# Row maxima of the first phase in small groups inside the matmul tasks, in an adaptive-norm block with softmax attention

## The chip, the cores and the metric

The kernel runs on one core of a Trainium2 chip. The metric is the device time of one execution in microseconds; lower is better. TensorE is called PE, VectorE DVE, ScalarE ACT, GpSimd POOL, and SP is the engine that issues most DMAs.

## What is computed

A block with adaptive layer norm on 2048 tokens of width 448: a softmax attention of 16 heads (28 wide each), then an MLP of width 1792, both scaled and shifted by rows made from a conditioning vector. All of it is in float32.

```python
mod = (_silu(c) @ w_mod).reshape(c.shape[0], 6, 1, -1)
sa, ca, ga, sb, cb, gb = (mod[:, i] for i in range(6))
h = _layernorm(x) * (1 + ca) + sa
q, k, v = split(h @ wqkv)                      # 16 heads of 28
p = _softmax(q @ k^T * 28 ** -0.5)             # 2048 x 2048 per head
x = x + ga * ((p @ v) @ wo)
h = _layernorm(x) * (1 + cb) + sb
x = x + gb * (gelu(_layernorm(h) @ w1 + b1) @ w2 + b2)
```

## The kernel before

**Precision.** Each float32 operand is split into a high and a low part, and a product is three products of parts. A projection of 448 input channels is therefore eleven accumulating matmuls (`terms448`, issued by `mm_acc`).

**Two phases of attention.** The first phase makes queries, keys and values; the second makes scores, exponentials and the weighted sums. The softmax needs a maximum of each row before the exponentials. It is not found from the final scores, but ahead of them, from a product of the high parts alone: for group `g` of four heads, query tile `qt` (512 queries), key block `cch` (512 keys), a quarter `i` of the queries (128) and head `j`, `max_mm` multiplies 128 queries by 512 keys (L466) into one PSUM buffer, and DVE reduces that to one column (`max_one`, L471). There are 1024 such maxima. Head `j` uses rows 32j to 32j+27 of the PE array, its *row group*, so matmuls of four different `j` run at the same time.

When all 64 maxima of a query tile are there (`count`, with the counter `left`), `max_fin` reduces them and later a call `put` transposes them on DVE (L509) and writes them by four DMAs (L512) into an extra row of the query tile, beside the 28 rows of each head. The score matmuls of that tile (L1162) read that row, so the maximum is subtracted by the matmul itself.

**Pairs.** For the first group of heads and query tiles 1 to 3, the key blocks 0 and 1 are taken together: `pair_diff` multiplies the queries by the difference of the two key blocks (`k_diff`), ACT applies a Relu to that (L479) into one of three tiles of slot `d0`, and a second matmul with key block 0 (`rest`) is combined with it on DVE (L483). So one pair takes two matmuls, one ACT read and one DVE read and gives two maxima. There are 48 pairs.

**The order of the first phase.** It runs over four blocks `b` of 512 tokens, and in each over a list of tasks: query and key projections (`qk_task`), value projections (`v_task`), each eleven matmuls into one of two `pa` buffers, and between them the transposes and the affine step of the next block (`h_chunk`, L267) and, in block 1, the modulation matmuls (L630). The order of every engine's instructions is the order in which this code issues them. Maxima that have become possible wait in two lists: `mxq` for single ones, `pxq` for pairs. They are sorted so that those of head group 0 and query tile 0 come first, then head group 1, then the rest of group 0.

The maxima are issued by `emit_task` behind each task: four or five operations, sometimes a sixth (`P1RATE`, `p1_n`), with both matmuls of one to three pairs in the same call. In five tasks `emit_mid` issues four more halfway through the eleven matmuls. Their PSUM buffers are a ring of five (`mx_ring`: two `ma`, two `m2`, one `m1`); a sixth operation uses the buffer `o`.

**The border.** Behind the loop's last task (the sixteenth value projection is left for attention step 0) `finish_max(0, 0)` issues whatever maxima the first query tile still lacks, and `tick_late(True)` calls its `put`. Then the PSUM pools are changed over and the second phase starts. It has 256 steps (16 units of head group and query tile, 16 key tiles each), and each step issues the remaining maxima too (`emit_max`), three or four per step by the rule in `n_maxima`. In the last four units, steps 8 to 11 also carry part of the output projection; there the number follows from how many maxima are left over.

Of the kernel before, what the change touches and what calls it, by code (L numbers as in the profile page):

```python
# [26 lines left out]
NC = 4  # L27
# [2 lines left out]
NKT = S // 128  # L30
NFT = F // 128
NTT = S // 128
P1RATE = 4
YTAGS = [f"{a}{i}" for a in ("kh", "qh") for i in range(4)]
EPS = 1e-5
SCALE = float(DH) ** -0.5
# [3 lines left out]
def tile_adaln_block(ctx: ExitStack, tc: tile.TileContext, x, wqkv, wo, w1, b1, w2, b2, c, w_mod, out):  # L40
# [338 lines left out]
            )  # L379
        sp.dma_start(ones_d.rearrange("j (q n) -> j q n", n=256), ones[:, None, :].broadcast_to([4, 8, 256]))  # L380

    def mm_acc(p, terms, mid=None):
        for i, (a, b) in enumerate(terms):
            if mid and i == len(terms) // 2:
                mid()
            pe.matmul(p, a, b, start=(i == 0), stop=(i == len(terms) - 1))  # L386


# [16 lines left out]
    def qk_task(b, kind, g, begun=None):  # L405
        p, ts = begun or qk_terms(b, kind, g)
        if begun is None:
            mm_acc(p, ts, p1_n[3])
        emit_task(*p1_n[:3])
        if g == 0:  # L410
            tg = ("kh" if kind else "qh") + str(b)
            hi = sb.tile([128, 512], F32R, tag=tg, name=nm(tg), bufs=1)
            (kh_sb if kind else qh_sb)[(g, b)] = hi
        elif g == 1 and b < 2:

            hi = sbt("raw" if kind else "osb", [128, 512], F32R, bufs=3 if kind else 2)
            (kh_sb if kind else qh_sb)[(g, b)] = hi
        else:
            hi = sbt("hi", [128, 512], F32R, bufs=3)
        full = sbt("full", [128, 512], bufs=3)  # L420
        lo = sbt("lo", [128, 512], F32R, bufs=3)
        act.copy(full, p)

        def split():
            (act.copy if b else dve.tensor_copy)(hi, full)
            if kind == 1 and (g, b) == (0, 1):
                k_diff.append(sbt("raw", [128, 512], F32R, bufs=3))
                pool.tensor_tensor(out=k_diff[0], in0=f(hi), in1=f(kh_sb[(0, 0)]), op=ALU.subtract)
            pool.tensor_tensor(out=lo, in0=full, in1=f(hi), op=ALU.subtract)
            sl = slice(b * 512, (b + 1) * 512)  # L430
            for part, t in enumerate((hi, lo)):
                sp.dma_start(f(dscr[kind][part][g])[:, sl], f(t))

            if b < 3 or g == 0 or (kind, g) == (0, 1):
                put_spare()
            spare.append((kind, g, sl))

        return split

    def v_task(b, t, p):  # L440
        ts = slice(t * 128, (t + 1) * 128)
        hh, hl = hT[b]
        mm_acc(p[:, :D], terms448(
            lambda k: hh(k)[:, ts], lambda k: hl(k)[:, ts], lambda k: wv[0][:, k, :], lambda k: wv[1][:, k, :],
        ), p1_n[3] if phase1[0] else None)
        if phase1[0]:
            emit_task(*p1_n[:3])
        act.copy(v_sb[b][:, t, :, :DH], p[:, :D].rearrange("p (h d) -> p h d", d=DH))


# [2 lines left out]
    mxq = []  # L453
    pxq = []
# [68 lines left out]
    phase1 = [True]  # L523
# [49 lines left out]
            count(g, qt, [cch])  # L573


    def emit_task(n, sixth, n_pairs):
        if not n:
            return
        pairs = [pxq.pop(0) for _ in range(min(n_pairs, len(pxq)))]
        rests = [pair_diff(*m) for m in pairs]  # L580
        js = [m[3] for m in pairs]
        n_ops = n - len(pairs) + (sixth and len(pairs) > 0)
        singles = []
        for x in range(n_ops - len(pairs)):
            if mxq:

                free = [j for j in range(4) if j not in js] or range(4)
                fits = [y for y, m in enumerate(mxq[:16]) if m[:3] == mxq[0][:3] and m[4] == free[x % len(free)]]
                singles.append(mxq.pop(fits[0] if fits else 0))
        ops = [lambda ps, m=m: max_one(*m, ps) for m in singles]  # L590
        ops[2:2] = rests
        for x, op in enumerate(ops):
            op(ps_o if x + len(pairs) == 5 else ps_mx)
        for g, qt, cch, i, j in singles:
            count(g, qt, [cch])
        for g, qt, i, j in pairs:
            count(g, qt, [0, 1])


    def emit_mid():  # L600
        for j in range(4):
            fits = [x for x, m in enumerate(mxq[:16]) if m[4] == j]
            if fits:
                m = mxq.pop(fits[0])
                max_one(*m)
                count(*m[:2], [m[2]])

    p1_n = [0, False, 1, None]

    def finish_max(g, qt):  # L610
        while left[(g, qt)] > 0:
# [72 lines left out]
    for n, i in (  # L684
# [7 lines left out]
        p, ts = firsts[n]  # L692
# [3 lines left out]
    for b in range(NB):  # L696
        more = b + 1 < NB
        tasks = []
# [10 lines left out]
        for n, (tb, kind, g) in enumerate(tasks):  # L709
            post = []  # L710
            ready, newq = newq, []
            if not more and n == len(tasks) - 2:

                mx_ring[:] = ["ma", "ma", "m2", "m2", "m1"]
            p1_n[0] = P1RATE if b < 1 else P1RATE + 1
            if not more and n == len(tasks) - 1:
                p1_n[0] = 0

            k = n - (6, 4, 4, 4)[b]
            p1_n[1] = not (more and (0 <= k < NC)) and not (b == 1 and n < 4)  # L720
            p1_n[2] = (3 if n > 4 else 1) if b == 3 else 2 if b == 2 and p1_n[1] else 1
            p1_n[3] = emit_mid if (b, n) in ((1, 1), (1, 3), (1, 5), (1, 7), (2, 8)) else None
            if kind < 2:
                fn = qk_task(tb, kind, g, firsts[n] if b == 0 and n < 3 else None)
                if g == 0:
# [571 lines left out]
```

## Time and profile before

| | |
|---|---|
| median of 3 runs | 1129.84 us (1128.42 to 1130.21) |
| the profiled execution's own time | 1130.08 us |
| its span, first to last instruction | 1128.0 us |
| first phase, from its first full task to the first score matmul | 24.54 to 169.21 us |
| attention steps | 169.21 to 834 us |
| MLP | 834 us to the end |

The page gives busy time per engine, a row of tenths over the span, the chain of work that ended last, and groups of instructions by line of the source, engine and tile. The order of time shows single instructions or merged rows of equal ones: start, time from the first one's start to the last one's end, engine, line, operation, tile written and tiles read, and in brackets the idle time ahead of it and what ended that. `PE` rows are matmuls and `PEld` rows the weight loads that belong to them; matmuls overlap, so the distance from start to start is what one costs in a row of them.

### The profile page before, as it was taken

To read this page: it belongs to the slowest core of one execution; us is meant where nothing else is said; L and a number is where in the kernel's file an instruction comes from. 1 tells how busy PE (TensorE), PEld (TensorE's weight loads), DVE (VectorE), ACT (ScalarE), POOL (GpSimd) and SP (SyncE) were. 2 spreads that over 40 slices of the span, in tenths; PEclk is the share of its full clock that TensorE was granted. 3 is DMA by queue.
4 is the path that set the end of the run, shared out by engine and by line. 5 is a ranking of instruction groups with operands and counts; after the bars stand their busy time and mean duration, and the time that the engine had idled before them with its cause. 6 is when DMAs were issued, how large, how long until landed. Compare 5 with 4: busy or idle time off the path is not lost.

```text
span 1128.0 us, 20665 instructions
## 1 busy us (share of the span) xinstructions
PE 1116.4 (99%) x8319; PEld 670.1 (59%) x8319; DVE 843.7 (75%) x1485; ACT 672.0 (60%) x823; POOL 209.6 (19%) x211
## 2 busy tenths in 40 slices
PE   8999999999999999999999999999999999999998
PEld 6756674444444444444444454545468888888887
DVE  6968788999999999999999978595448853444322
ACT  4555657888887888788788867576752321111110
POOL 1533332110000000000000020217114504123000
PEclk9999999999999999999999999999999999999999
DMA  9562263121121211311111312020422100000000
GB/s 303 202 200 88 91 200 114 48 84 41 58 95 57 58 40 57 91 53 58 53 44 58 112 41 83 4 85 1 137 73 78 35 33 1 1 33 1 33 1 33
DMA packets 49341, 81.19 MB, mean 72 GB/s; under 512 B 12311, under 2 KB 18702, under 8 KB 49234
## 3 DMA queue, kind: packets, MB, share of 16 engines
q1 hardware_dynamic: 48762, 79.14, 22.1%
q8 instruction: 65, 1.06, 0.4%
q10 hardware_dynamic: 148, 0.46, 0.1%
q0 software_dynamic: 336, 0.28, 0.1%
q14 instruction: 30, 0.25, 0.1%
HBM read 55.04 MB, written 26.48 MB: 72 GB/s over the span
## 4 chain that ended last, share of the span: by engine, by line
PE 94%; DVE 3%; ACT 1%; DMA 1%; issue 1%; POOL 0%; SPq 0%; DVEq 0%; ACTq 0%; POOLq 0%
PE s L1162 26%; PE o L1132 22%; PE m L386 16%; PE pa L386 8%; PE m L466 6%; PE s L1232 3%; PE s L1233 3%; PE s L1231 3%; DVE mxp L471 2%; PE t L1232 1%; PE t L1233 1%; PE t L1231 1%; DMA slot_c<-in_w_mod_dram 1%; PE ma L466 1%; PE o L267 1%
## 5 line engine op out<-in xcount | busy, mean ns | idle before, releaser
L471 DVE TENSOR_REDUCE mxp<-m 128x1 f32<-128x512 f32 x884 | 568.8, 686 | 75.3 <-PE m L466 41.1
L1162 PE MATMUL s<-slot_b,slot_a 28*128 28x512 f32 (+1 forms) x3072 | 376.3, 420 | 0.0
L1162 PEld LDWEIGHTS s<-slot_b,slot_a 28*128 28x128 f32 (+1 forms) x3072 | 213.0, 184 | 247.4 <-ACT slot_c L1167 124.1
L466 PE MATMUL m<-kh,qh 28*128 28x512 f32 x863 | 287.6, 472 | 1.2 <-DVE mxp L471 0.9
L1167 ACT ACTIVATE slot_c<-s 128x1024 f32<-128x1024 f32 x170 | 174.3, 1025 | 75.9 <-PE s L1162 75.6
L1132 PE MATMUL o<-slot_c,v 128*32 128x512 f32 x680 | 178.8, 605 | 0.0
L1208 ACT ACTIVATE full<-m,b_col 128x512 f32<-128x512 f32 x56 | 38.6, 689 | 192.0 <-PE m L386 175.5
L1132 PE MATMUL o<-slot_c1h,v 128*32 128x512 f32 x512 | 134.7, 605 | 0.0
L1132 PE MATMUL o<-slot_c0h,v 128*32 128x512 f32 x512 | 134.7, 605 | 0.0
L1167 ACT ACTIVATE slot_c0h<-s 128x1024 f32<-128x1024 f32 x128 | 130.4, 1019 | 2.4 <-PE m L386 2.4
L1167 ACT ACTIVATE slot_c1h<-s 128x1024 f32<-128x1024 f32 x128 | 130.4, 1019 | 0.0
L1211 DVE CAST hi<-full 128x512 fp32r<-128x512 f32 x56 | 25.5, 455 | 134.6 <-ACT full L1208 134.6
L466 PEld LDWEIGHTS m<-kh,qh 28*128 28x128 f32 x863 | 114.3, 182 | 8.6 <-DVE mxp L471 5.1
L1167 ACT ACTIVATE slot_d<-s 128x1024 f32<-128x1024 f32 x86 | 88.1, 1025 | 39.3 <-PE s L1162 39.1
L895 POOL TENSOR_TENSOR osb<-osb,osb 128x512 f32<-128x512 f32 x16 | 20.9, 1307 | 441.1 <-DMA osb<-drec 356.8
L1132 PE MATMUL o<-slot_d,v 128*32 128x512 f32 x344 | 90.5, 605 | 0.4 <-ACT osb L1101 0.4
L386 PE MATMUL m<-y,slot_a 128*128 128x512 f32 x160 | 60.7, 395 | 0.0
L1132 PEld LDWEIGHTS o<-slot_c,v 128*32 128x32 f32 x680 | 24.5, 108 | 52.4 <-issue 49.5
L1212 DVE TENSOR_TENSOR lo<-full,hi 128x512 fp32r<-128x512 f32 x56 | 44.2, 788 | 5.9 <-DVE hi L1211 0.9
L471 DVE TENSOR_REDUCE mxp<-ma 128x1 f32<-128x512 f32 x54 | 35.6, 683 | 7.1 <-PE m L466 4.8
L386 PE MATMUL m<-y,slot_v 128*128 128x512 f32 x112 | 39.2, 396 | 0.0
L386 PE MATMUL m<-y,slot_b 128*128 128x512 f32 x112 | 39.0, 398 | 0.0
(316 smaller groups left out, 1626.7 us busy)
## 6 DMA issues: line engine op xcount, KB each, us to landing
slot_b<-d SPq DMA_DIRECT2D x32, 256.0 KB
slot_a<-d SPq DMA_DIRECT2D x32, 256.0 KB
d<-lo SPq DMA_DIRECT2D x28, 256.0 KB
d<-hi SPq DMA_DIRECT2D x16, 256.0 KB
osb<-drec SPq DMA_DIRECT2D x15, 256.0 KB
out_dram<-xn SPq DMA_DIRECT2D x16, 224.0 KB
raw<-in_B_w_dram SPq DMA_DIRECT2D x14, 224.0 KB
qh<-d SPq DMA_DIRECT2D x12, 256.0 KB
```

The source lines that it names most:

```text
L386: pe.matmul(p, a, b, start=(i == 0), stop=(i == len(terms) - 1))
L466: pe.matmul(m, qh_sb[(g, qt)][js, i * 128 : (i + 1) * 128], k[js, :], start=True, stop=True)
L471: dve.tensor_reduce(out=mxp[(g, qt)][:, i, j, cch : cch + 1], in_=m, op=ALU.max, axis=AX.X)
L1132: pe.matmul(o[32 * j : 32 * j + 32, :], v_sb[kt // 4][:, kt % 4, 4 * g + j, :], p[j // 2][:, j % 2, :], start=(kt == 0), stop=(kt == NKT - 1),
L1162: pe.matmul(s2[:, jj, :], ks[rows_, kp, kc], qs[rows_, qp, :], start=(term == 0), stop=(term == 2))
L1167: act.activation(pt[hf], s2, AF.Exp, scale=SCALE)
L1208: act.activation(gf, p, AF.Gelu_apprx_tanh, bias=b1_col[:, i : i + 1])
L1211: dve.tensor_copy(ghi, gf)
L1212: dve.tensor_tensor(out=glo, in0=gf, in1=f(ghi), op=ALU.subtract)
L1231: pe.matmul(pp, ghi[:, ts], w_hi, start=(m == 0), stop=False)
L1232: pe.matmul(pp, ghi[:, ts], w_lo, start=False, stop=False)
L1233: pe.matmul(pp, glo[:, ts], w_hi, start=False, stop=(m == NFT - 1))
```

## The change

`emit_task`, `emit_mid` and their rates are replaced. `emit_visit` issues at most one maximum per row group: first the second matmuls of the pairs that the last visit opened, counted as taken row groups, then up to two new pairs (three open or closing at a time), then single maxima for the row groups that are left. `visit_due` is called ahead of every matmul of a task's eleven and makes a visit once six (while pairs are waiting or open) or nine (otherwise) matmuls have passed. In a visit the new pairs' difference matmuls are issued first, then the second matmuls of the older pairs, then the single ones. The loop's last task but one opens no new pairs, and the last has no visits.

```diff
-P1RATE = 4
+PAIR_GAP, ONE_GAP = 6, 9
...
-    def mm_acc(p, terms, mid=None):
+    def mm_acc(p, terms, visits=False):
         for i, (a, b) in enumerate(terms):
-            if mid and i == len(terms) // 2:
-                mid()
+            if visits:
+                visit_due()
             pe.matmul(p, a, b, start=(i == 0), stop=(i == len(terms) - 1))
...
         if begun is None:
-            mm_acc(p, ts, p1_n[3])
-        emit_task(*p1_n[:3])
+            mm_acc(p, ts, True)
...
-        ), p1_n[3] if phase1[0] else None)
-        if phase1[0]:
-            emit_task(*p1_n[:3])
+        ), phase1[0])
...
-    def emit_task(n, sixth, n_pairs):
-        if not n:
-            return
-        pairs = [pxq.pop(0) for _ in range(min(n_pairs, len(pxq)))]
-        rests = [pair_diff(*m) for m in pairs]
...
-    def emit_mid():
+    px_open = []
+
+    def emit_visit(n_new):
+        rests = px_open[:]
+        px_open.clear()
+        js = [m[3] for m, _ in rests]
+        for _ in range(min(n_new, 3 - len(rests))):
+            fits = [x for x, m in enumerate(pxq[:8]) if m[3] not in js]
+            if fits:
+                m = pxq.pop(fits[0])
+                js.append(m[3])
+                px_open.append((m, pair_diff(*m)))
+        for (g, qt, i, j), rest in rests:
+            rest(ps_mx)
             count(g, qt, [0, 1])
         for j in range(4):
             fits = [x for x, m in enumerate(mxq[:16]) if m[4] == j]
-            if fits:
+            if fits and j not in js:
                 m = mxq.pop(fits[0])
                 max_one(*m)
                 count(*m[:2], [m[2]])
 
-    p1_n = [0, False, 1, None]
+    p1_n = [0, 0]
+
+    def visit_due():
+        p1_n[1] += 1
+        if p1_n[0] is not None and p1_n[1] > (PAIR_GAP if pxq or px_open else ONE_GAP):
+            p1_n[1] = 1
+            emit_visit(p1_n[0])
...
-            p1_n[0] = P1RATE if b < 1 else P1RATE + 1
-            if not more and n == len(tasks) - 1:
-                p1_n[0] = 0
-            k = n - (6, 4, 4, 4)[b]
-            p1_n[1] = not (more and (0 <= k < NC)) and not (b == 1 and n < 4)
-            p1_n[2] = (3 if n > 4 else 1) if b == 3 else 2 if b == 2 and p1_n[1] else 1
-            p1_n[3] = emit_mid if (b, n) in ((1, 1), (1, 3), (1, 5), (1, 7), (2, 8)) else None
+            p1_n[0] = (2, None if n == len(tasks) - 1 else 0)[not more and n >= len(tasks) - 2]
```

The lines of the code move by some three to twelve: what is L466, L471, L479, L483, L502, L509, L512, L1132 and L1162 before is L463, L468, L476, L480, L499, L506, L509, L1120 and L1150 after. L386 stays.

More of the change, by code (lines that the diff above doesn't have):

```diff
@@ L573, in emit_max @@
             count(g, qt, [cch])
-    def emit_task(n, sixth, n_pairs):
-        if not n:
-            return
-        pairs = [pxq.pop(0) for _ in range(min(n_pairs, len(pxq)))]
-        rests = [pair_diff(*m) for m in pairs]
[L581 to L596, printed above, removed]
+    px_open = []
[11 more added lines that the diff above has]
+            rest(ps_mx)
             count(g, qt, [0, 1])
-    def emit_mid():
         for j in range(4):
             fits = [x for x, m in enumerate(mxq[:16]) if m[4] == j]
-            if fits:
+            if fits and j not in js:
                 m = mxq.pop(fits[0])
```

## The prediction

> **What bounds the kernel now.** I read the page first, then busy time by window, then the order of time on TensorE (PE) around the maxima of the first phase.
>
> ```profile
> span 1128.0 us, 20665 instructions
> PE 1116.4 (99%) x8319; PEld 670.1 (59%) x8319; DVE 843.7 (75%) x1485; ACT 672.0 (60%) x823; POOL 209.6 (19%) x211
> PE 94%; DVE 3%; ACT 1%; DMA 1%; issue 1%; POOL 0%; SPq 0%; DVEq 0%; ACTq 0%; POOLq 0%
> 24.54:169.21 144.67, 144.00 (x730) 98.69 (x729) 118.35 (x251) 86.36 (x157) 58.63 (x61) 1.00 0.49 158
> 169.21:834.00 664.79, 662.32 (x6144) 308.68 (x6144) 567.20 (x937) 515.91 (x550) 85.15 (x86) 1.00 0.21 64
> ```
>
> The chain that ended last is 94% PE, so what counts is what PE's in-order stream is made to do or wait for. The columns of the last two lines are the stretch, its length, then busy time of PE, PEld, DVE, ACT and POOL, the granted clock and DMA. The first phase runs from 24.54 us to 169.21 us and takes 144.67 us; there DVE is busy 118.35 us and ACT 86.36 us, so both have room on average, and the question is whether they have it at the right moment. The changed kernel's instruction order differs in that phase, in what crosses its end, and in nine steps near the end of attention.
>
> **Breaking the stream.** In the order of time on PE, L386 are the accumulating matmuls (eleven to a task), L466 the matmuls for the maxima, L630 a foreign group behind a task:
>
> ```profile
> 64.65 1.20 PE L386 MATMUL pa<-slot_c,slot_a 128*128 128x512 f32 x4
> ...
> 66.14 0.62 PE L386 MATMUL pa<-slot_c,slot_a 128*128 128x512 f32 x2
> 66.61 0.40 PE L386 MATMUL pa<-slot_c1h,slot_a 128*128 128x512 f32 x1
> ...
> 67.39 0.49 PE L466 MATMUL ma<-raw,qh 28*128 28x512 f32 x1
> ...
> 68.05 0.96 PE L630 MATMUL o<-slot_v,slot_d 128*32 128x448 f32 x8
> 68.94 1.19 PE L386 MATMUL pa<-slot_c,slot_a 128*128 128x512 f32 x4
> ...
> 70.29 0.50 PE L466 MATMUL ma<-kh,qh 28*128 28x512 f32 x1
> ...
> 70.72 0.50 PE L386 MATMUL pa<-slot_c0h,slot_a3h 128*128 128x512 f32 x1
> ...
> 72.29 0.49 PE L466 MATMUL ma<-raw,qh 28*128 28x512 f32 x1
> ...
> 73.37 0.50 PE L466 MATMUL m<-raw,osb 28*128 28x512 f32 x1
> 73.80 0.58 PE L630 MATMUL o<-slot_v,slot_d 64*32 64x448 f32 x4
> ```
>
> Two matmuls take 0.47 us (66.14 to 66.61), so 0.23 us each and 2.54 us for eleven; the unbroken eleven take 2.74 us (64.65 to 67.39). The 0.20 us over is what it costs to enter and leave a block. The task at 68.94 has a group of four in its middle and takes 3.35 us to 72.29: the group costs 0.61 us, break included. A group of five behind a task, unstalled, takes 0.66 us (67.39 to 68.05), break excluded.
>
> By the instruction order, the first phase has 209 maxima matmuls before: 13 groups of four and 28 of five or six. After, it has 218: 54 groups of four and a last one of two. At these prices that is 13 x 0.61 + 28 x 0.86 = 32.0 us against 54 x 0.61 + 0.33 (the pair of maxima at 169.22, below) = 33.3 us, +1.3 us. Besides, in 15 places a group stood between a task and its transposes or modulation matmuls, and shared their break; now it lies inside a block and those break the stream by themselves. The trace shows no transposes straight behind an accumulating block, so I bound that break by 0 and 0.20 us, and take the 0.20 that a block's ends cost everywhere else: +3.0 us. **PE work: +4.3 us (1.3 to 4.5).**
>
> **Stalls that go.** The group at 72.29 needs 1.51 us (to 73.80) instead of 0.66: its last matmul waits until 73.37 for a buffer that DVE still reads, because another group of four was put in 2 us earlier. The old code does that in five tasks: 5 x 0.85 = 4.3 us. What L466 waited for in the whole phase is in the answer on that line:
>
> ```profile
> its engine sat idle before it (us, times) until:
>   DVE mxp L471: 7.2, 22
> ```
>
> So between 4.3 and 7.2 us; with the small waits of the sixth matmuls counted I take **-6.6 us**.
>
> **Stalls that come.** A group of four now comes every six matmuls while pairs are open (6 x 0.23 + 0.61 = 2.0 us) and every nine otherwise (2.7 us), through five buffers: a group may start when the first three results of the one before it have been read. In a pair, the first half is read by ACT (L479), and ACT is in order:
>
> ```profile
> 110.07 0.59 ACT L479 ACTIVATE slot_d<-m 128x512 f32<-128x512 f32 x1
> 110.56 0.58 ACT L479 ACTIVATE slot_d0h<-m 128x512 f32<-128x512 f32 x1
> 111.03 0.58 ACT L422 COPY full<-pa 128x512 f32<-128x512 f32 x1
> 111.50 0.78 ACT L223 ACTIVATE xn<-acc,nm,rs 128x448 f32<-128x448 f32 x1
> 112.17 0.43 ACT L224 ACTIVATE xn<-acc,nm,rs 128x64 f32<-128x64 f32 x1
> 112.50 0.61 ACT L425 CAST hi<-full 128x512 fp32r<-128x512 f32 x1
> ```
>
> Before, the reads of a pair stand ahead of the task's copy, normalisation and cast. After, a group early in the next task finds them queued: 0.47 + 1.00 + about 0.5 = 2.0 us from the task's end, then 0.49 + 0.59 us for two reads, so the second buffer comes free some 3.2 us after the task's end. A group that starts with the task has its successor 2.0 us later: 1.2 us of stall. Block 2 has the normalisation in its first four tasks; there the groups come 0, 0.4, 0.6 and 0.8 us into the task (one matmul later each time), and the stall shrinks by as much, with what each delays: about 1.2 + 1.0 + 0.7 + 0.4 = 3.3 us. In block 1 the modulation matmuls lengthen the tasks and hide all but 0.5 us.
>
> DVE's turn is where no pairs are open. Its own pitch, from the next fence, is 1.20 us for two maxima (149.75 to 150.95), so 2.4 us of each 2.7 us; in the tasks of the value projection (448 columns) the nine matmuls are shorter, and the layer statistics of the next block, or the splits of block 0, also stand in DVE's queue. Over the six groups ahead of block 2's pairs I count some 2 us of DVE work more than PE gives it room for; over the eight groups of block 0, where DVE is nearly full already, 0.8 us. A stall here gives ACT time, so block 2's first stall shrinks by about 1 us. **Stalls that come: 3.3 - 1.0 + 0.5 + 2.1 + 0.8 = +5.7 us (2 to 10).** Nothing is queued behind a stalled matmul but the rest of PE's stream, and PE's stream is the chain.
>
> **The end of the phase.** This decides. The score matmuls need the row maxima of the first query tile, block (0,0), as an extra row of the queries, put there by four DMAs. Before, the last of its 64 maxima comes three tasks ahead of the end; after, a group with an open pair has room for one or two single maxima only, and two of the tile's are left to the call that finishes it (`finish_max`), right ahead of the first score matmul. The price is that of the same chain earlier, from the trace:
>
> ```profile
> 149.75 1.29 DVE L471 TENSOR_REDUCE mxp<-m 128x1 f32<-128x512 f32 x2 [0.27 <-PE m L466]
> 150.95 0.68 DVE L483 CUSTOM_DVE_ANT_0 slot_d0h<-ma,slot_d0h 128x512 f32<-128x512 f32 x1
> ...
> 163.25 0.22 DVE L502 TENSOR_REDUCE m<-mxp 128x16 fp32r<-128x64 f32 x1
> 163.57 0.21 DVE L509 STREAM_TRANSPOSE full<-m 128x32 f32<-128x32 f32 x1
> 163.81 2.33 SPq L512 DMA_DIRECT2D slot_b<-full  x4
> ...
> 169.21 0.49 PE L1162 MATMUL s<-slot_b,slot_a 29*128 29x512 f32 x2
> 169.22 0.51 PE L466 MATMUL m<-kh,qh 28*128 28x512 f32 x2
> 169.54 0.85 PE L1162 MATMUL s<-slot_b,slot_a 28*128 28x512 f32 x6
> 169.78 2.48 DVE L471 TENSOR_REDUCE mxp<-m 128x1 f32<-128x512 f32 x4 [0.58 <-PE m L466]
> ```
>
> From the two matmuls to DVE's first read 0.56 us (169.22 to 169.78); two reads 1.29; the reduction and the transposition to the first issue 0.60 (163.21, where the maximum ahead ends, to 163.81); four issues 2.33 us; and the last one's landing, which is between 0 and 3.07 us, since the scores start at 169.21 and wait for nothing. I take 1.5, the middle. Together 6.3 us, of which PE would have used 0.33 (169.22 to 169.54): **+5.9 us (4.4 to 7.5)**. Behind the waiting score matmul stand all of step 0 and the last value task; ahead of the four issues on SP stand the key loads, which wait for a task that ends three tasks earlier, so I add nothing for them. DVE is idle for 0.58 us at this point before, too, so the pause gives nothing back later.
>
> **Attention.** Nine maxima fewer remain. By the order, the steps without projection keep their three and four; nine of the twelve projection steps fall from three to two, and the list runs empty at the same step. A step with three against one with none:
>
> ```profile
> 716.56:721.35 4.79, 4.79 (x36) 3.19 (x36) 1.92 (x4) 2.51 (x4) 1.15 (x1) 1.00 0.00 0
> 816.89:821.43 4.54, 4.54 (x34) 2.86 (x33) 1.60 (x4) 2.50 (x5) 1.14 (x1) 1.00 0.18 58
> ```
>
> 0.25 us for three: 0 to 0.25 each, **-0.9 us (0 to -2.2)** at 0.1 each.
>
> **Sum.** 4.3 - 6.6 + 5.7 + 5.9 - 0.9 = +8.4 us against the profiled execution's own 1130.08 us. That stands 0.24 us over the median of 1129.84 us, so 1138.2 us.
>
> **Rivals.** *The border costs more, by the clock.* A PE that has stood still for 5.9 us may start slowly again. The start of the kernel shows it: the same matmul, before and after.
>
> ```profile
> 1.36 3.75 PE L301 MATMUL pa<-ident 128*128 128x128 f32 x16 [1.36 <-POOL cst L117]
> 5.30 1.38 PE L301 MATMUL pa<-ident 128*128 128x128 f32 x10
> ```
>
> 0.23 us each at first, 0.14 from 5.30 on, and 1.00 granted in each window above. If the pause brings the slow rate back for as long as at the start (3.9 us), half of it is lost: 1.9 us, 1140.1 us. The Trainium skill, "TensorE: Matmul & The Clock Gate", Part 1, says that the clock falls to half after an idle window of about 3.4 us and needs about as long to recover; the start agrees, no pause inside this trace is long enough to test it, and by that rule the pause forecast here would do it in most runs.
>
> *Stalls compound.* If ACT and DVE lag together in block 2 and a stall comes with every group, some 10 us come instead of 5.7: 1142.5 us, or 1144.4 with the clock. For it: DVE's 118.35 us of 144.67. Against it: in a pair group DVE reads only two or three results.
>
> *Faster.* The one mechanism is that the border wait is hidden and the stalls that come are half as large: 4.3 - 6.6 + 2.9 - 0.9 = -0.3 us, and with transposes that need no break of their own -3.3 us: 1126.5 us. It decides if the two last maxima were not in front of the scores, that is, if the wait fell below about 2.5 us; the order puts them there, and 2.33 us of issue alone fill that.
>
> *It does not do what it says.* Groups with one maximum per row group are what the order shows, so I give this nothing.
>
> **How the numbers follow.** Forecast 0.55, slower clock 0.24, compounding stalls 0.10, faster 0.06, cancelling to within 0.2% (2.3 us, about what a measurement of this kernel can tell) 0.05. Range 1133.0 to 1145.0 us: the low end takes the border at 4.4, free transposes and stalls of 4 (1.3 - 6.6 + 4 + 4.4 - 0.5 = +2.6 us), with some spared; the high end is compounding with the slow clock. Faster 0.06, same 0.05, slower 0.89.
>
> **What would show it.** In the profile after, PE should be idle 5 to 7 us ahead of the first score matmul, with the put's issues straight before it; the first phase up to that idle time should take 146 to 150 us; groups of four should take 0.43 us between neighbours where unstalled, with stalls ahead of L466 in block 2's first four tasks, ended by ACT; projection steps should be shorter by 0 to 0.25 us. A first phase under 143 us, or scores that start at once, would make the prediction wrong.

## The result, and the profile after

The changed kernel takes 1143.47 us (median of 4 runs, 1142.63 to 1144.41) against 1129.88 us for the kernel before in runs beside it: ratio 1.0123, 95% interval 1.0105 to 1.0141. It is slower by 13.6 us; +8.4 us was forecast. The profiled execution of the changed kernel took 1144.41 us, 14.3 us over that of the kernel before. Line numbers have moved: the maxima are L463 (DVE's reads of them L468, the Relus of the pairs L476, the combination L480), the put L506 and L509, the score matmuls L1150; L386 is the same.

From the page, the span, the shares of the chain that ended last, and the group of the score matmuls, whose last part is the idle time ahead of them and what ended it:

```profile
span 1142.3 us, 20679 instructions
PE 90%; DVE 4%; DMA 2%; ACT 1%; issue 1%; POOL 1%; SPq 0%; DVEq 0%; ACTq 0%; POOLq 0%
L1150 PE MATMUL s<-slot_b,slot_a 28*128 28x512 f32 (+1 forms) x3072 | 376.1, 420 | 5.7 <-DMA slot_b<-full 5.6
```

PE's share of the chain falls from 94% to 90%, and the score matmuls, which waited for nothing before, wait 5.6 us for the DMA that writes the row maxima. Busy time by window (stretch, length, busy PE, PEld, DVE, ACT, POOL, granted clock, DMA share, GB/s), for the first phase, the wait, attention steps 0 and 1, the other steps, and the MLP:

```profile
25.17:175.38 150.21, 149.46 (x738) 98.17 (x737) 119.42 (x256) 91.10 (x164) 58.68 (x61) 1.00 0.49 162
175.38:181.52 6.14, 0.49 (x4) 0.21 (x3) 1.72 (x4) 0.53 (x1) 0.00 (x0) 0.82 0.13 46
181.52:191.10 9.58, 9.04 (x52) 5.78 (x52) 5.71 (x9) 4.02 (x5) 3.11 (x4) 0.76 0.36 103
191.10:844.29 653.19, 651.00 (x6057) 302.72 (x6054) 555.77 (x919) 508.54 (x541) 82.14 (x82) 1.00 0.20 62
844.29:1142.30 298.01, 293.18 (x1380) 249.99 (x1376) 142.73 (x262) 60.74 (x98) 62.48 (x51) 1.00 0.08 26
```

The 14.3 us are: 5.5 in the first phase (150.21 for 144.67), 6.1 in the wait, 2.1 in attention (181.52 to 844.29 is 662.8 us; up to the same score matmul, which starts at 829.89 there, it is 660.7 before), 0.6 because the first full task starts that much later (25.17 for 24.54; in the other kept traces it starts between 23.3 and 25.7), and nothing in the MLP. The clock column is the new thing: 0.82 in the wait and 0.76 in the two steps behind it. Cut finer, the same column shows 1.00 up to 179 us, 0.50 from 179.5 to 186 and 1.00 again from 187 on. At half rate for the part that is missing, that is 2 x 0.18 x 6.14 = 2.2 us and 2 x 0.24 x 9.58 = 4.6 us, so the clock was halved for some 6.8 us, beginning 3.9 us into the window of the wait, which is 3.4 us after PE's last matmul ended. The order of time at the border:

```profile
175.38 0.50 PE L463 MATMUL m<-kh,qh 28*128 28x512 f32 x2
175.91 1.29 DVE L468 TENSOR_REDUCE mxp<-m 128x1 f32<-128x512 f32 x2 [0.66 <-PE m L463]
177.23 0.22 DVE L499 TENSOR_REDUCE m<-mxp 128x16 fp32r<-128x64 f32 x1
177.56 0.21 DVE L506 STREAM_TRANSPOSE full<-m 128x32 f32<-128x32 f32 x1
177.80 2.32 SPq L509 DMA_DIRECT2D slot_b<-full  x4
...
181.52 0.79 PE L1150 MATMUL s<-slot_b,slot_a 29*128 29x512 f32 x2 [5.64 <-DMA slot_b<-full]
...
183.85 1.86 PE L386 MATMUL m<-slot_e,slot_c 128*128 128x448 f32 x4
```

This is the chain that was forecast, link by link. The last row is the sixteenth value projection in step 0: its matmuls stand 0.4 us apart, where those of the last task ahead of the border stand 0.2 us apart.

### The profile page after: what moved, and what is told of

Read it like the earlier page. It is cut to its first block, busy times and chain, and to the rows that moved or that the text cites. A ratio compares the mean times of both kernels' runs of the same rounds, so it can differ in the third digit from the quotient of the medians.

```text
span 1142.3 us, 20679 instructions
## 1 busy us (share of the span) xinstructions
PE 1124.1 (98%) x8319; PEld 671.0 (59%) x8319; DVE 840.5 (74%) x1485; ACT 676.8 (59%) x830; POOL 209.7 (18%) x211
## 4 chain that ended last, share of the span: by engine, by line
PE 90%; DVE 4%; DMA 2%; ACT 1%; issue 1%; POOL 1%; SPq 0%; DVEq 0%; ACTq 0%; POOLq 0%
PE s L1150 26%; PE o L1120 22%; PE m L386 16%; PE pa L386 7%; PE m L463 6%; PE s L1220 3%; PE s L1221 3%; PE s L1219 3%; DVE mxp L468 2%; PE t L1220 1%; PE t L1221 1%; PE t L1219 1%; PE ma L463 1%; DMA slot_c<-in_w_mod_dram 1%; DMA drec<-den 1%
## 5 line engine op out<-in xcount | busy, mean ns | idle before, releaser
L468 DVE TENSOR_REDUCE mxp<-m 128x1 f32<-128x512 f32 x884 | 568.4, 685 | 78.4 <-PE m L463 50.2
L1150 PE MATMUL s<-slot_b,slot_a 28*128 28x512 f32 (+1 forms) x3072 | 376.1, 420 | 5.7 <-DMA slot_b<-full 5.6
L1150 PEld LDWEIGHTS s<-slot_b,slot_a 28*128 28x128 f32 (+1 forms) x3072 | 213.6, 184 | 252.7 <-ACT slot_c L1155 124.2
L463 PE MATMUL m<-kh,qh 28*128 28x512 f32 x873 | 290.6, 474 | 1.0 <-DVE mxp L468 0.7
L1120 PE MATMUL o<-slot_c,v 128*32 128x512 f32 x680 | 178.9, 605 | 0.0
L1120 PE MATMUL o<-slot_c1h,v 128*32 128x512 f32 x512 | 134.7, 605 | 0.0
L1120 PE MATMUL o<-slot_c0h,v 128*32 128x512 f32 x512 | 134.7, 605 | 0.0
L463 PEld LDWEIGHTS m<-kh,qh 28*128 28x128 f32 x873 | 115.8, 182 | 9.9 <-DVE mxp L468 4.4
L1120 PE MATMUL o<-slot_d,v 128*32 128x512 f32 x344 | 90.5, 605 | 0.4 <-ACT osb L1089 0.4
L386 PE MATMUL m<-y,slot_a 128*128 128x512 f32 x160 | 60.7, 395 | 0.0
L1120 PEld LDWEIGHTS o<-slot_c,v 128*32 128x32 f32 x680 | 24.5, 108 | 53.0 <-issue 49.7
L386 PE MATMUL m<-y,slot_v 128*128 128x512 f32 x112 | 39.2, 396 | 0.0
L386 PE MATMUL m<-y,slot_b 128*128 128x512 f32 x112 | 39.0, 397 | 0.0
L1221 PE MATMUL s<-slot_v,lo 128*128 128x448 f32 x96 | 35.0, 365 | 0.0
```

What stands on the lines that cost most here:

```text
L463: pe.matmul(m, qh_sb[(g, qt)][js, i * 128 : (i + 1) * 128], k[js, :], start=True, stop=True)
L468: dve.tensor_reduce(out=mxp[(g, qt)][:, i, j, cch : cch + 1], in_=m, op=ALU.max, axis=AX.X)
L1120: pe.matmul(o[32 * j : 32 * j + 32, :], v_sb[kt // 4][:, kt % 4, 4 * g + j, :], p[j // 2][:, j % 2, :], start=(kt == 0), stop=(kt == NKT - 1),
L1150: pe.matmul(s2[:, jj, :], ks[rows_, kp, kc], qs[rows_, qp, :], start=(term == 0), stop=(term == 2))
L1221: pe.matmul(pp, glo[:, ts], w_hi, start=False, stop=(m == NFT - 1))
```

## The experiments

Theory: the loss is three separate things, the wait at the border with the clock behind it, stalls in the first phase behind ACT and DVE, and extra maxima there that give nothing back later. The rivals are told with each run. The ratios are to executions of the kernel before that ran beside each run; their medians lie between 1128.9 and 1129.9 us, so differences below 1 us between medians of different runs say little, and the kept traces are used where they can tell more.

### The border alone

**One new pair a visit in block 3.** The two maxima of query tile 0 that are left to the border were crowded out by open pairs.

```diff
-            emit_visit(p1_n[0])
+            emit_visit(min(p1_n[0], 1) if p1_n[2] and mxq and mxq[0][:2] == (0, 0) else p1_n[0])
...
+            p1_n[2] = b == 3
```

> The changed kernel, but in block 3 a group opens one new pair instead of two as long as the first query tile lacks maxima, so that this tile is complete about 8 us ahead of the border and its put is issued two tasks earlier. Theory (the wait at the border and the slow clock behind it make up most of the loss): the 6.1 us of idle PE and the half clock of 6.8 us both go, some 8 us: 1135 to 1137 us. Rival A (the wait only shows up at the border, and the scores would wait there for key loads or DVE anyway): within 2 us of 1143.5. Rival B (only the waiting counts, the slow clock hides behind ACT and DVE): about 1137.5, with 1.00 clock all the same.

Measured: 1136.33 us (1134.81 to 1137.45), ratio 1.0063 (1.0048 to 1.0078), 7.1 us less than the changed kernel (6.3 us less if each is taken against the kernel before beside it), as the theory had it. In the order of time the put now stands ahead of the last task, and the scores follow the projection at once:

```profile
168.91 2.38 SPq L509 DMA_DIRECT2D slot_b<-full  x4
...
173.65 0.57 PE L386 MATMUL pa<-slot_e,slot_c0h 128*128 128x448 f32 x2
174.15 0.50 PE L1151 MATMUL s<-slot_b,slot_a 29*128 29x512 f32 x2
```

Its window of steps 0 and 1:

```profile
174.15:182.26 8.11, 7.46 (x53) 4.50 (x52) 5.64 (x9) 4.55 (x6) 0.00 (x0) 1.00 0.73 222
```

That is 8.11 us at clock 1.00, for 9.58 at 0.76. The first phase takes as long as in the changed kernel (150.18 us for 150.21), so the gain is the border's. The border costs about 7 us: the wait and some 1.5 us of clock.

**The kernel before with its last two maxima held back.** The same from the other side.

```diff
-                mxq.append((g, qt, cch, i, j))
+                (held if (g, qt, cch, i) == (0, 0, 3, 3) and j > 1 else mxq).append((g, qt, cch, i, j))
...
+    mxq[:0] = held
     finish_max(0, 0)
```

> The kernel before, with two single maxima of the first query tile held back to the call at the border, and nothing else changed. Theory (the border alone costs 8 us: 6 of wait, 2 of half clock): 1137 to 1138.5 us. Rival A (the wait is hidden where the old first phase leaves DVE and SP less to do): 1130 to 1132. Rival B (wait without the clock): 1135.5 to 1136.5.

Measured: 1136.95 us (1135.95 to 1138.88), 1.0067 (1.005 to 1.0084): 7.9 us for two maxima in the wrong place, with nothing else changed. That is just under the theory's 1137 and over rival B's 1136.5; the trace, which is of the longest of the four executions (1138.88 us), shows the half clock that rival B leaves out. Windows of its wait and of the two steps behind it:

```profile
168.84:174.96 6.12, 0.50 (x4) 0.22 (x3) 1.72 (x4) 0.53 (x1) 0.00 (x0) 0.93 0.33 119
174.96:185.90 10.94, 10.63 (x52) 6.46 (x53) 5.74 (x9) 4.41 (x5) 3.15 (x5) 0.66 0.37 102
```

The wait is as long (6.12 us), but here the clock falls later in it, 5.2 us into the window, and comes back 5.9 us into the steps. In this execution it falls a second time, for 3.4 us from 184.3 on, without such a pause ahead. So the two steps take 10.94 us, and that is more than the price of the pause alone.

**The clock apart from the wait.** 50, and in a second run 24, matmuls of the identity with itself, with no use for their result, fill the wait of the changed kernel.

```diff
     tick_late(True)
+    busy = ps_s()
+    for _ in range(50):
+        pe.matmul(busy[:, :128], ident, ident, start=True, stop=True)
```

> The changed kernel with 50 small matmuls on the identity, read by nobody, between the last two maxima and the first score matmul, so that PE is busy through most of the wait. If the idle time brings the half clock, it stays at 1.00 and steps 0 and 1 lose their extra 1.5 to 2 us: 1141.2 to 1142 us. Rival (the clock falls for another reason, or the steps are late because of DVE and ACT): 1143 to 1144, or later if the small matmuls outlast the wait.

Measured with 50: 1147.09 us (1146.77 to 1148.51), 1.0162 (1.0147 to 1.0177). The clock stayed at 1.00 and step 0 took 4.72 us instead of 6.12, but each of these matmuls stands in the trace as two, the hundred took 11.4 us, and the scores came late. So this run couldn't give the price, and the next has fewer.

> The changed kernel with 24 matmuls of the identity with itself, not 50, in the wait for the first query tile's row maxima; at two passes of 112 ns each they take 5.4 us and end inside the wait. If the half clock behind the pause costs what the first step showed (6.12 us at half clock, 4.72 at full), the time is 1143.5 - 1.4 = 1142.1 us (1141.4 to 1142.7), with the clock at 1.00 throughout. Rival: the slower matmuls are hidden behind the Exps of the first steps and the time stays at 1143.2 to 1143.8.

Measured with 24: 1141.87 us (1140.67 to 1143.38), 1.011 (1.0093 to 1.0127). In the order of time the 48 matmuls of the trace end as the scores start:

```profile
176.18 5.62 PE L781 MATMUL pa<-ident 128*128 128x128 f32 x48
...
181.96 0.49 PE L1153 MATMUL s<-slot_b,slot_a 29*128 29x512 f32 x2
```

And the window of steps 0 and 1:

```profile
181.96:190.12 8.16, 7.40 (x55) 4.31 (x55) 5.65 (x9) 4.03 (x5) 3.10 (x4) 1.00 0.41 113
```

The wait is still there, the two steps take 8.16 us at full clock. Keeping PE busy with nothing is worth 1.4 us in the trace (8.16 for 9.58): the price of the half clock. The medians, 1.6 us apart (1.0 us against the kernel before beside each), agree but could not show it by themselves, since the two ranges overlap. The half clock is not hidden behind the Exps of the first steps, as the rival had it. The Trainium skill ("TensorE: Matmul & The Clock Gate", Part 1) says that PE falls to half rate after an idle window of about 3.4 us and needs about as long of work to recover. The traces agree with it roughly: the fall came 3.4 us after the last matmul's end in the changed kernel and 4.7 us after it in the kernel before with two maxima held back, and recovery took 4.6 and 5.9 us of work.

### The stalls of the first phase

**The split's first copy on POOL.** In block 2 the Relus of a pair were forecast to queue behind the task's copy, normalisation and cast on ACT. The edit takes the cast away from ACT in blocks 1 and 2.

```diff
-            (act.copy if b else dve.tensor_copy)(hi, full)
+            (pool.tensor_copy if b in (1, 2) else act.copy if b else dve.tensor_copy)(hi, full)
```

> The changed kernel with the cast to the high part moved from ACT to POOL in the query and key tasks of blocks 1 and 2. If the stalls in block 2's pairs come from the first half of a pair waiting behind copy, normalisation and cast on ACT, each of the four shrinks by about 0.5 us: 1141 to 1142 us, and ACT's first read starts 0.5 us earlier behind the task. Rival (DVE holds the buffers, as the releaser column says): no change, 1143 to 1144. POOL's longer chain to the stores could cost something later: up to 1145.

Measured: 1140.03 us (1138.96 to 1143.7), 1.0103 (1.0086 to 1.012), 3.4 us less, which is more than the theory's range. By the traces the first phase is 2.7 us shorter (147.46 for 150.21): 0.8 us of it are stalls of block 1, for which nothing had been forecast, and 2.0 us stalls of block 2's pairs. The order of time in block 2 of the changed kernel, with the weight loads (PEld) inside the group:

```profile
113.16 0.61 ACT L424 CAST hi<-full 128x512 fp32r<-128x512 f32 x1
113.67 1.08 ACT L476 ACTIVATE slot_d0h<-m 128x512 f32<-128x512 f32 x2
...
113.84 0.50 PE L463 MATMUL m<-raw,qh 28*128 28x512 f32 x1
...
114.31 0.18 PEld L463 LDWEIGHTS m<-kh,qh 28*128 28x128 f32 x1 [0.29 <-ACT slot_d0h L476]
...
114.79 0.18 PEld L463 LDWEIGHTS m<-kh,qh 28*128 28x128 f32 x1 [0.30 <-ACT slot_d0h L476]
...
114.85 0.69 DVE L480 CUSTOM_DVE_ANT_0 slot_d0h<-m,slot_d0h 128x512 f32<-128x512 f32 x1 [1.03 <-PE m L463]
115.22 0.50 PE L386 MATMUL pa<-slot_b,slot_a 128*128 128x512 f32 x1
```

The same place with the cast on POOL:

```profile
111.00 1.07 ACT L476 ACTIVATE slot_d0h<-m 128x512 f32<-128x512 f32 x2
...
111.63 0.50 PE L463 MATMUL m<-raw,qh 28*128 28x512 f32 x1
...
112.55 0.50 PE L386 MATMUL pa<-slot_b,slot_a 128*128 128x512 f32 x1
...
114.14 0.18 PEld L463 LDWEIGHTS ma<-raw,qh 28*128 28x128 f32 x1 [0.37 <-DVE mxp L468]
...
114.57 0.73 PE L386 MATMUL pa<-slot_b,slot_a 128*128 128x512 f32 x2
```

In the changed kernel the Relus start when the cast ends (113.67), and the next group of four takes 1.38 us (113.84 to 115.22) instead of 0.43, while DVE waits 1.03 us for PE. Without the cast in front, the same group takes 0.92 us. ACT's queue is the cause, and the loads inside the group name it. The summary for the maxima's line L463 in the changed kernel seems to say otherwise: of the idle time ahead of them it puts 11.5 us, in 34 places, down to DVE's reads. But 26 of these 34 are the first weight load of a group, and such a load has 0.30 to 0.37 us of idle time ahead of it even where the group is not held up at all (114.14 above: four maxima in 0.43 us). Inside the groups DVE ends 8 idle times (2.5 us) and ACT 7 (2.2 us); with the cast on POOL it is DVE 8 (2.4 us) and ACT 2 (0.5 us).

**Both edits.** 

> The changed kernel with both earlier edits: one new pair a visit in block 3 while the first query tile is open, and the split's first copy on POOL instead of ACT in blocks 1 and 2. If the wait at the border (7.1 us by the first edit) and the waits for the Relus behind those copies (3.4 us by the second) are separate, both gains add: 1136.3 - 3.4 = 1132.9 us (1131.5 to 1134.5), with no pause ahead of the first score matmul. Rival: the second edit's gain was in part work that slid into the pause at the border; then without the pause less of it is left: 1135 to 1136.5 us.

Measured: 1131.72 us (10 runs, 1130.07 to 1136.03), 1.0026 (1.0016 to 1.0035), 4.6 us less than with the first edit alone. The two gains are separate, as the theory had it: in the traces the first phase is 2.6 us shorter than with the first edit alone (147.54 for 150.18), and without that edit it was 2.7. What the medians show above that is not placed.

**Wider spacing in block 0.** On top of the first edit, twelve matmuls instead of nine between the visits of block 0.

```diff
-        if ... p1_n[1] > (PAIR_GAP if pxq or px_open else ONE_GAP):
+        if ... p1_n[1] > (PAIR_GAP if pxq or px_open else 12 if p1_n[2] is None else ONE_GAP):
```

> The changed kernel with one new pair a visit in block 3 while the first query tile is open (1136.3 us), and in block 0 a visit behind every twelve matmuls instead of every nine. If the 2.0 us of stalls in block 0 come from DVE, which has four maxima to do in each visit beside the splits and the normalisation and falls behind at a visit per nine matmuls, the wider spacing takes most of them: 1134.5 us (1133.8 to 1135.3), and the fifth to eighth projections of the block start at most 1 us later than in the kernel before, not 2.7. Rival: the stalls come from DVE's other work of these two projections, wherever the maxima stand: 1135.8 to 1136.8 us, and the fifth projection again starts 2.5 us or more late.

Measured: 1136.52 us (1134.76 to 1139.24), 1.0066 (1.0049 to 1.0082): no gain, the rival's number. The sixth projection was 1.7 us late against the kernel before instead of 2.7, but the first visit now came one matmul into the second task, where the keys were not yet split:

```profile
28.43 0.50 PE L463 MATMUL ma<-kh,qh 28*128 28x512 f32 x2 [0.81 <-DVE kh L424]
```

So the spacing did help, and the shift of the phase paid most of it back: the first phase takes 149.83 us for 150.18. The rival's reason is in part in the traces: in the changed kernel DVE first does a part of the value weights' split (L185, 1.32 us from 33.00) and a cast (0.41 us from 34.24), and only then reads the group before the one at 34.93. The trace of this run is of its longest execution (1139.24 us); in it the clock was halved for 6.8 us from 716 us on, far from the edit, so its total is not used here.

### The count of maxima

**As many as before.** Both edits, and `ONE_GAP` at 10 instead of 9. The first phase then has 208 maxima (216 with both edits, 209 before), and every attention step the kernel before's number, but for one or two at the end of the list.

> The changed kernel with one new pair a visit in block 3 while the first query tile is open and the first copy of the split on POOL in blocks 1 and 2 (1131.72 us), and a visit behind ten instead of nine matmuls where no pairs are open: 208 maxima in the first phase instead of 216 (the kernel before has 209), and the attention's steps have the kernel before's counts. If what is left of the loss is work that the attention did for nothing, two groups of 0.61 us go and the steps of the output products take as long with three as with two: 1131.7 - 1.2 = 1130.5 us, and down to 1129.3 if the waits for DVE in block 0 shrink as well. Rival: those steps do gain from fewer maxima, so that the eight cost there what they save here: 1131.3 to 1132.5 us.

Measured: 1128.71 us (11 runs, 1128.0 to 1130.64), 0.9999 (0.9989 to 1.0008): no difference from the kernel before, and below both ranges. The gain is 3.0 us, more than the 1.2 for two groups of maxima; the wider spacing also takes stalls away. By the traces the first phase is 2.5 us shorter than with both edits (145.0 for 147.54), and the groups' time beyond the unstalled 0.43 us falls by 1.6 us (6.8 to 5.1). The order of time in block 0 of the changed kernel:

```profile
34.93 0.88 PE L463 MATMUL m<-kh,qh 28*128 28x512 f32 x2
35.18 1.27 DVE L468 TENSOR_REDUCE mxp<-ma 128x1 f32<-128x512 f32 x2
35.91 1.09 PE L463 MATMUL ma<-kh,qh 28*128 28x512 f32 x2
36.38 0.67 DVE L468 TENSOR_REDUCE mxp<-m 128x1 f32<-128x512 f32 x1
36.93 1.43 PE L386 MATMUL pa<-slot_b,slot_a 128*128 128x512 f32 x5
...
38.43 0.63 PE L386 MATMUL pa<-slot_b,slot_a 128*128 128x512 f32 x2
38.90 0.60 PE L267 MATMUL o<-ident,xn 128*128 128x128 f32 x4
```

And of this one:

```profile
34.67 0.49 PE L463 MATMUL m<-kh,qh 28*128 28x512 f32 x2
34.73 1.09 PE L463 MATMUL ma<-kh,qh 28*128 28x512 f32 x2
...
35.75 0.50 PE L386 MATMUL pa<-slot_b,slot_a 128*128 128x512 f32 x1
```

A group of four takes 2.00 us (34.93 to 36.93) in the changed kernel, since DVE still reads the group before it, and 1.08 us at a spacing of ten. That the extra maxima of the first phase bring nothing in attention shows in the windows of the four steps with output product in unit 12. The kernel before, with three maxima in each:

```profile
661.66:678.89 17.23, 17.23 (x132) 10.48 (x128) 8.18 (x13) 10.15 (x12) 3.43 (x3) 1.00 0.00 1
```

The changed kernel, with two:

```profile
675.60:692.88 17.28, 17.28 (x129) 10.19 (x126) 5.59 (x9) 10.18 (x12) 3.44 (x3) 1.00 0.00 1
```

DVE's count (13 and 9) shows the four maxima that are gone; the time is the same within 0.05 us. With ten matmuls between visits and three maxima again, the same steps take 17.24 us.

### Is there something better in it?

**The visits in block 1 alone.** From the first projection of block 1 to the start of block 2's list of tasks the changed kernel was 3.5 us faster than the kernel before; 2.7 us of that lie in block 1's own list, to which the edit applies (44.7 us for 47.4). So: the kernel before, with `visit_due` in block 1 only. The first phase then has 202 maxima.

```diff
+            if b == 1:
+                p1_n[0], p1_n[3] = 0, visit_due
```

> The kernel before, with the changed kernel's visits in block 1 alone; blocks 0, 2 and 3 keep the groups at the end of each projection. Between the start of block 1 and the start of block 2 the changed kernel gained 3.5 us on the kernel before. If that gain is block 1's own and the seven maxima that go to the attention instead cost as little as the nine fewer there brought (about nothing), the time is 1129.0 - 3.5 = 1125.5 us (1124.5 to 1127). Rival: the gain is paid for by these seven maxima, at 0.43 us of TensorE each: 1128 to 1129.5 us.

Measured: 1129.56 us (10 runs, 1128.78 to 1133.57), 1.001 (0.9999 to 1.002). The rival's number. The trace is of the longest execution, 4.0 us over the median. The windows of its first phase and of its first unit (16 steps):

```profile
24.69:166.38 141.69, 140.75 (x724) 96.56 (x723) 112.80 (x243) 88.48 (x160) 58.65 (x61) 1.00 0.50 163
166.38:213.01 46.63, 45.10 (x388) 20.64 (x387) 41.05 (x72) 31.28 (x34) 10.06 (x12) 0.96 0.26 74
```

The first unit of the kernel before:

```profile
169.21:211.59 42.38, 41.97 (x382) 20.01 (x381) 37.70 (x64) 31.30 (x34) 10.07 (x12) 1.00 0.29 81
```

The first phase did gain 3.0 us (141.69 for 144.67); the first unit, where the planner put the missing maxima (64 instead of 58), gave back 4.25 in this execution. Part of that is a half clock of 3.4 us (the 0.96; last section), which can cost up to 1.7 us; the rest, some 2.5 us, is 0.43 us for each of the six maxima, which was the rival's price. In a group of the first phase one maximum costs 0.15 us (0.61 for four).

**The missing maxima in the output-product steps.** 

> The kernel before with the visits in block 1 alone, as in the last such run (1129.56 us; its first phase 141.69 us against 144.67, but its first score unit 46.63 us with 64 maxima against 42.36 with 58), and with the attention's planner allowed four instead of three maxima in the steps of the output products of units 12 to 14, so that the six extra maxima stand there and not in the first unit. If steps of that kind have room, as in the changed kernel, where two maxima took as long as three, the first phase's gain stays: 1129.3 - 3.0 = 1126.3 us (1125.3 to 1127.3). Rival: a fourth maximum costs these steps what it costs a score step (2.74 - 2.15 = 0.59 us): 1126.3 + 6 x 0.59 = 1129.8 us.

```diff
-        return 4 if plain[0] % 2 or (over > 3 * n_wo and over > 0) else 3
+        return 4 if plain[0] % 2 or (over > 4 * n_wo and over > 0) else 3
```

Measured: 1129.53 us (12 runs, 1128.12 to 1131.14; the kernel before beside it 1128.91), ratio 0.9996 (0.9986 to 1.0006): no difference. The rival again. The window of the same four steps of unit 12, with four maxima each:

```profile
658.71:677.78 19.07, 18.77 (x136) 11.19 (x133) 10.73 (x19) 10.15 (x12) 3.42 (x4) 1.00 0.01 1
```

19.07 us for 17.23: these steps hold three for nothing, and the four more cost 1.84 us. The first unit, with 58 maxima again, takes 42.41 us. The kernel before already stood at the edge.

**With the copy on POOL as well.** 

> The same kernel, with the split's first copy on POOL instead of ACT in blocks 1 and 2. In the changed kernel that took 0.8 us out of block 1 and 2.5 us out of block 2. If the Relu pairs behind these copies hold up TensorE in the same way with the visits of block 1: 0.8 us less than without it, 1125.5 us (1124.5 to 1126.6). Rival: POOL, which also does the difference behind each copy, is late with both, the splits' transfers land later and later blocks wait: 1126.3 to 1128 us.

Measured: 1128.68 us (12 runs, 1128.06 to 1130.79), 0.9997 (0.9989 to 1.0006). That is 0.8 us less than without it, the gain that was forecast, though a gain of this size in the medians is within their spread; the time itself lies outside both ranges, because the run without the edit was not as fast as its theory had it. The traces agree with the gain: time beyond 0.43 us for a group of four and 0.66 us for one of five or six adds up to 4.2 us without the edit and 3.4 us with it.

**Eight matmuls between visits in block 1**, the planner's old limit and the copy on POOL. 

> The kernel before with visits in block 1 alone and the first copy of the split on POOL in blocks 1 and 2, as in the last run of that kind (first phase 141.15 us against 144.67), but with a visit behind eight instead of nine matmuls where no pairs are open, so that the first phase has 206 maxima instead of 202, and with the planner's old limit of three maxima in the output-product steps of units 12 to 14. If a maximum costs TensorE the same wherever it stands, except in those steps, which have room for three: the first phase takes 141.15 + 0.61 = 141.8 us, the first unit two maxima more than before, 42.36 + 2 x 0.59 = 43.5 us, the output-product units what they take in the kernel before; 1128.9 - 2.9 + 1.2 = 1127.2 us (1126.3 to 1128.2). Rival: at eight matmuls DVE, which needs 2.4 us for four maxima, falls behind and the tighter visits give their stalls back: 1128.5 to 1130 us.

Measured: 1128.43 us (11 runs, 1127.53 to 1130.15), 0.9992 (0.9984 to 1.0001). Between theory and rival, and not to be told from the kernel before. Windows of the first phase and the first unit:

```profile
23.90:167.30 143.40, 142.37 (x728) 97.13 (x727) 115.24 (x247) 81.32 (x146) 67.12 (x75) 1.00 0.49 160
167.30:210.41 43.11, 42.19 (x384) 19.81 (x383) 38.80 (x68) 31.28 (x34) 10.07 (x12) 1.00 0.28 80
```

The first unit costs what was forecast (43.11 us for 43.5), but the first phase gains 1.3 us instead of 2.9: the tighter visits give part of block 1's gain back (the time beyond 0.43 and 0.66 us per group is 5.4 us, for 3.4 at a spacing of nine). A version that beats the kernel before by more than the measurement can tell was not found.

## Why the prediction was right, and where its sum was off

The direction, the range and the place that decides were right: the two maxima left to the border cost 7.1 us when they are put right in the changed kernel, and 7.9 us when they alone are put wrong in the kernel before. But the case that was given 0.55 is not the one that came. The measured time lies near the upper end of the range, next to the 1144.4 us that the prediction worked out for two of its rivals together, the slow clock (0.24) and stalls of some 10 us (0.10). The sum came out 5.9 us below the profiled execution's +14.3, term by term:

- **The border, +5.9.** Measured 6.14 - 0.33 = 5.8 us, by the same links: 0.53, 1.32, 0.57, 2.32 us, and 1.40 us for the last landing, where the guessed middle of 0 to 3.07 was 1.5. That this link came so close is luck.
- **The clock, a rival at 0.24.** It happened in all three kernels with that pause whose PE was left idle (the changed kernel, the one with the cast on POOL, and the kernel before with two maxima held back). This is the step that failed by its weight: a pause of 6 us was forecast and the half clock behind it not made part of the likeliest case. Its price was put at 1.9 us; the short filling measures 1.4 in the trace. The start of the kernel, from which the price was taken, is a weak witness: the matmuls there go from 0.23 to 0.14 us, but the profile's granted clock is 1.00 from 1.36 to 5.30 us as well.
- **Stalls that come, +5.7 (2 to 10).** Counted in the trace of after, groups of four beyond 0.43 us add up to some 9.3 us: 2.0 in block 0 (0.8 forecast), 1.3 in block 1 (0.5), 1.9 ahead of block 2's pairs (2.1), 2.8 in block 2's pairs (2.3), and 1.3 later, where none was forecast. The mechanisms hold (ACT's queue by the run with the cast on POOL; DVE in block 0 by the rows at 34.93), the sizes were low where DVE is nearly full. The rival of compounding stalls had the size but not the way: 19 of the 54 groups are held up, in block 2's pairs every other one. "Ended by ACT" was right as a sign to look for: inside these groups ACT is named (114.31, 114.79).
- **Stalls that go, -6.6.** Counted the same way in the trace of before, beyond 0.43 us for a group of four and 0.66 us for one of five or six, they add up to 6.7 us, 4.4 of it in the five tasks with a group in their middle (4.3 forecast). The upper bound of 7.2 us was no measure of stalls, since that answer also counts the idle time ahead of the first weight load of groups that were not held up.
- **PE work, +4.3 (1.3 to 4.5).** What the first phase's +5.5 leaves beside these stalls is 5.5 - 9.3 + 6.7 = +2.9. That the transposes need less than the 0.20 us taken is shown: from the last two accumulating matmuls to the first transpose 0.47 us pass (38.43 to 38.90), two matmuls' own time. The 0.20 us itself was high: 0.47 / 2 x 11 is 2.59 us, not 2.54, and a projection that follows another without a break takes 2.57 us in the trace of after (25.17 to 27.74), so a break costs some 0.17. Without a break for the transposes the sum would be 1.3; where the other 1.6 us lie stays open. This term came out too high and hid part of what the stalls were too low.
- **Attention, -0.9.** Nothing was gained: two maxima take as long as three (17.28 and 17.23 us). The row used compared a step with three to one with none in another unit. Beside the clock, attention is 0.65 us longer; the last unit, which has no maxima, takes 0.8 us more than before, but it takes between 43.4 and 45.3 us over the kept traces whatever the kernel, so I give that to no cause.

Of the other signs, the idle time (5.64 us) fits, the first phase of 150.21 us lies just over the 146 to 150 us that were named, and the projection steps are no shorter.

That the loss is made of these parts is shown by taking them back one after another. Against the kernel before beside each, it is 13.6 us, 7.3 without the wait at the border and the half clock behind it, 2.4 with the cast off ACT, and -0.4 with the count and the spacing of ten, which is the kernel before's time. In that last step the first phase loses 2.5 us, of which two groups fewer are 1.2 and fewer stalls 1.6 by their own counts, 0.3 more than the whole.

## What to carry to other kernels

When work is spread more evenly, look first at who needs the last piece of it: two items that slip past a phase's end cost more than everything that the new spacing changed inside it. Price a move at both its ends, since one more maximum cost 0.15 us in the first phase, about half a microsecond in one attention step and nothing in another that still had room. And where a forecast puts a pause of some microseconds on TensorE, put the slower clock behind it into the sum.

## What the runs showed of the hardware that was not expected

The granted clock also fell with no long pause ahead. In the run with the visits in block 1 alone, windows of steps 1 and 2 of its first unit:

```profile
171.07:175.25 4.18, 3.63 (x26) 1.25 (x22) 3.76 (x6) 3.21 (x4) 0.00 (x0) 0.86 0.62 200
175.25:178.58 3.33, 3.33 (x28) 1.64 (x25) 2.46 (x4) 1.64 (x2) 2.84 (x4) 0.66 0.18 52
```

By the clock column that is 1.2 + 2.3 = 3.4 us at half rate, in and behind a step in which PE was idle for 0.55 us in all. It is not the only place: the clock falls again in that execution at 713 us for 3.4 us, at 716 us for 6.8 us in the run with wider spacing in block 0, and at 184 us for 3.4 us in the kernel before with two maxima held back. PE waited 1.6 us at most ahead of these. All three traces are of the longest execution of their run, so such falls are part of why executions of one kernel differ. What triggers them was not tried. And a float32 matmul of 128 columns stands in the trace as two of 0.117 us each (48 in 5.62 us).
